# Six instead of four products of a seven-product tile with 512-column matmuls, in an attention and MoE kernel

## The chip, the cores and the metric

The kernel runs on one core of a Trainium2 chip. The metric is the device time of one execution in microseconds (us), as the median of several runs.

## The reference, cut to what is computed

```python
def _attn_ref(q, k, v, M_prev, z_prev, beta):            # q, k, v: 4 x 8 x 576 x 64
    a = softmax(causal(q @ k.T / sqrt(D)))
    local = a @ v
    q_p = elu(q) + 1
    mem_out = (q_p @ M_prev) / (q_p @ z_prev + 1e-6)
    g = sigmoid(beta)
    return g * mem_out + (1 - g) * local

def _moe_ref(x, w_in, w_out, s, b):                      # x: 2304 x 512, w_in: 512 x 2048, w_out: 2048 x 512
    r = np.maximum(x @ w_in, 0.0)
    return (s * (r * r) + b) @ w_out
```

The result of the attention, with its heads side by side, is the x of the second part. The "second product" below is the last one, with w_out; its left operand g = s r² + b is called G here.

## The kernel before

**Stages.** The attention and most of x @ w_in run first, interleaved by a planner. Then the rest of x @ w_in runs while w_out is read and split. The relu'd result r goes to DRAM (r_d) and comes back tile by tile. The last stage, 178 of 551 us, is the second product; the change is in it alone.

**Number format.** Every float32 operand X is split into H, its rounding to the matmul format (fp32r), and L = X - H. A product of A and B is the sum of three terms, H·BH + H·BL + L·BH, all added up in PSUM.

**Tiles and products.** The second product has nine tiles of 256 tokens. Each is cut 2 x 2 (tokens in halves of 128, the 2048 inner rows in halves of 1024, the 512 outputs in halves of 256) and done by a Strassen-Winograd scheme: seven products of 128 x 1024 x 256 instead of eight, with sums of blocks before (VectorE and GpSimd) and behind (VectorE). They go in the order `SEQ = [1, 7, 5, 6, 3, 2, 4]`. A product has eight steps f of 128 inner rows. Each product has one PSUM tile `yps` of two halves of 256 columns.

**Narrow and wide.** A product outside the tuple `WIDE` (narrow) takes three matmuls of 256 columns a step, H·BH (line 810), H·BL (L811) and L·BH (L812), all into the first half of its PSUM tile. A product in `WIDE` takes two: H times BH and BL side by side, 512 columns (L808), into both halves, and L·BH (L812) into the first half. The two halves are added afterwards: `onto` in `combine` runs one VectorE add from PSUM (L819) for a narrow product and two for a wide one. Product 1 has its own two instructions (L822 on ScalarE, L823 on VectorE) whichever it is.

**Left operands.** `operand(t, m, c)` makes the left operand of product m, once for each half c of the inner rows, two products ahead of its use in program order: a block sum in place (L790 for product 5 and L792 for product 6 on VectorE; L788 for product 7 and L794 for product 3 on GpSimd, into the buffer `sum`), the cast H (L795, ScalarE), and L (L796; on GpSimd for products 1, 2 and 4, on VectorE for 7, 5, 6 and 3). The tiles `op` have eight buffers, two to a product, so the operands of four products are there at most. The block sums work in place on the tile that was loaded (`src` for even tiles, `w1H` for odd ones), so L792 of the next tile's product 6 must come behind the GpSimd L796 of its product 1, which reads the block that L792 writes over. L794 needs L792's result, and L788 must come behind the VectorE L796 of product 3, which reads `sum`.

**What sets the order.** Each engine runs its instructions in the order of its own queue. In this stage the framework's scheduler, which works from a model of the times, arranges the queues; the code's order is what it starts from. TensorE's queue follows `SEQ`.

**The sums behind.** `combine` adds products 6, 7 and 5 into the running sums when product 6 is done, then 3, 2 and 4 when each is done. The sums behind product 4 of the last tile, and the DMA of the output after them, are the last work of the kernel.

Of the kernel before, what the change touches and what calls it, by code (L numbers as in the profile page):

```python
# [171 lines left out]
def attention_moe_kernel(  # L172
# [572 lines left out]
    def b_op(m, f):  # L745
        if m in LATE:
            return late[f // 4][:, f % 4, LATE.index(m)]
        return RB[f][:, PL[m]]
# [46 lines left out]
        nc.scalar.copy(H, x)  # L795
        (nc.gpsimd if m in ONPOOL else nc.vector).tensor_sub(L, x, H.bitcast(F32))  # L796

    WIDE = (1, 6, 3, 2)

    def product(t, m):  # L800
        OPS["ps", m] = tile = ps_y.tile([128, 2, NE], F32, tag="y", name="yps")
        ps = tile[:, 0]
        for f in range(KF):
            o = OPS[t, m, f // 4]
            H, L = o[:, 0, f % 4], o[:, 1, f % 4]
            B = b_op(m, f)
            if m in WIDE:
                nc.tensor.matmul(tile, lhsT=H, rhs=B, start=f == 0, stop=False)  # L808
# [5 lines left out]
    def combine(t, m):  # L814
        Y, U = YU[t % 2]

        def onto(y, x, n):
            for h in range(2 if n in WIDE else 1):
                nc.vector.tensor_add(y, y if h else x, OPS["ps", n][:, h])  # L819
# [133 lines left out]
```

## Time and profile before

| | |
|---|---|
| median of 3 runs | 554.07 us (554.06 to 554.45) |
| the profiled execution's own time | 552.9 us |
| its span, first to last instruction | 551.1 us |
| TensorE busy | 538.8 us, 98% of the span |
| VectorE, ScalarE, GpSimd busy | 395.4, 398.7, 274.1 us |
| mean granted TensorE clock | 0.994 of full speed |
| second product on TensorE | from 369.19 to 547.4 us |

In the profile PE is TensorE's matmuls, PEld its weight loads, DVE VectorE, ACT ScalarE, POOL GpSimd, and SP the engine that issues most DMAs. L with a number is a line of the kernel. A row of the timeline has its start, its duration, the engine, line and operation, what is written and read, and in brackets how long the engine had been idle before it and which instruction ended that. A VectorE instruction may start a little before the record of the one in front ends; the time from start to start is what a queue pays.

### The profile page before, as it was taken

What the parts mean: (1) busy time and instruction counts of PE and PEld (TensorE: products, weight loads), DVE (VectorE), ACT (ScalarE), POOL (GpSimd) and SP (SyncE); (2) the same over time, 40 slices, a digit from 0 to 9 for tenths busy, and PEclk for the clock granted to TensorE, in tenths of its full rate; (3) what the DMA queues carried; (4) which work ended last, traced back from release to release, by engine and by line L of the source; (5) the groups of instructions that cost most, each with busy time, mean ns of one, the idle gap of its engine ahead of it and who ended that gap; (6) DMA issues with size and microseconds to landing.
All of it is one profiled execution on the core that took longest, in us unless ns stands there. A gap on an engine that the chain in (4) does not pass through costs nothing.

```text
span 551.1 us, 11425 instructions
## 1 busy us (share of the span) xinstructions
PE 538.8 (98%) x4070; PEld 443.4 (80%) x4070; DVE 395.4 (72%) x971; ACT 398.7 (72%) x877; POOL 274.1 (50%) x279
## 2 busy tenths in 40 slices
PE   9898899999999999999999999999999999999997
PEld 6666577777777777776788888889999999999996
DVE  5999999999765445234009979353988898898893
ACT  5998799974788747647425658968988877977940
POOL 3773344556746663454000000326597678668781
PEclk9999799999999999999999999999999999999999
DMA  5645575745454342311149474648424435344011
GB/s 183 197 142 161 196 256 162 247 154 175 118 173 124 102 133 100 122 76 46 57 132 364 159 264 130 219 164 255 150 87 145 151 104 164 116 123 156 30 39 39
DMA packets 56665, 81.50 MB, mean 148 GB/s; under 512 B 7584, under 2 KB 39072, under 8 KB 56608
## 3 DMA queue, kind: packets, MB, share of 16 engines
q1 hardware_dynamic: 54064, 78.63, 44.0%
q10 hardware_dynamic: 2544, 2.14, 1.2%
q8 instruction: 32, 0.52, 0.4%
q14 instruction: 25, 0.20, 0.1%
HBM read 57.15 MB, written 23.59 MB: 147 GB/s over the span
## 4 chain that ended last, share of the span: by engine, by line
PE 90%; DVE 6%; ACT 1%; issue 1%; POOL 1%; DVEq 0%; POOLq 0%
PE yps L808 12%; PE yps L812 11%; PE sb L383 8%; PE sb L514 7%; PE tb L580 6%; PE hps L581 5%; PE hps L580 5%; PE hps L582 5%; PE tb L463 5%; PE tb L581 5%; PE tb L582 5%; PE yps L811 5%; PE yps L810 5%; PE sb L580 2%; DVE P L390 2%; PE sb L581 1%
## 5 line engine op out<-in xcount | busy, mean ns | idle before, releaser
L402 POOL TENSOR_SCALAR P<-P,sr,omg 128x576 f32<-128x576 f32 (+4 forms) x130 | 90.0, 707 | 57.1 <-DVE sr L436 31.1
L396 ACT ACTIVATE P<-P,mn 128x64 f32<-128x64 f32 (+4 forms) x160 | 89.1, 564 | 17.7 <-DVE mn L390 17.1
L812 PE MATMUL yps<-rb,op 128*128 128x256 f32 x360 | 101.1, 281 | 0.0
L390 DVE CUSTOM_DVE_ANT_0 P<-sb,mask 128x64 f32<-128x64 f32 (+4 forms) x160 | 71.6, 485 | 22.0 <-PE sb L383 21.9
L808 PE MATMUL yps<-rb,op 128*128 128x512 f32 x216 | 76.9, 396 | 0.0
L812 PEld LDWEIGHTS yps<-rb,op 128*128 128x128 f32 x360 | 67.9, 189 | 0.0
L788 POOL TENSOR_TENSOR sum<-src 128x512 f32<-128x512 f32 x10 | 13.0, 1296 | 103.5 <-ACT src L772 88.9
L383 PE MATMUL sb<-qk 64*128 64x288 f32 (+4 forms) x384 | 60.0, 419 | 0.4 <-DVE mn L390 0.4
L796 POOL TENSOR_TENSOR op<-src,op 128x512 fp32r<-128x512 f32 x30 | 44.5, 1505 | 16.8 <-ACT op L795 16.8
L463 PEld LDWEIGHTS tb<-ident,P 64*128 64x128 f32 x928 | 38.0, 141 | 17.0 <-issue 5.3
L463 PE MATMUL tb<-ident,P 64*128 64x64 f32 x928 | 44.4, 230 | 5.2 <-DVE xs L536 1.4
L383 PEld LDWEIGHTS sb<-qk 64*128 64x128 f32 x384 | 37.6, 193 | 13.4 <-issue 6.4
L808 PEld LDWEIGHTS yps<-rb,op 128*128 128x128 f32 x216 | 40.6, 188 | 9.0
L819 DVE TENSOR_TENSOR yu<-yu,yps 128x256 f32<-128x256 f32 x90 | 36.5, 414 | 14.6 <-PE yps L812 13.6
L795 ACT CAST op<-src 128x512 fp32r<-128x512 f32 x50 | 30.1, 617 | 16.2 <-DVE src L792 8.6
L810 PE MATMUL yps<-rb,op 128*128 128x256 f32 x144 | 40.5, 281 | 0.0
L811 PE MATMUL yps<-rb,op 128*128 128x256 f32 x144 | 40.5, 281 | 0.0
L796 DVE TENSOR_TENSOR op<-sum,op 128x512 fp32r<-128x512 f32 x36 | 38.3, 1065 | 0.9 <-ACT op L795 0.8
L472 ACT COPY pt<-tb 128x512 f32<-128x512 f32 x58 | 31.3, 591 | 7.6 <-PE tb L463 7.4
L796 POOL TENSOR_TENSOR op<-w1H,op 128x512 fp32r<-128x512 f32 x24 | 35.4, 1504 | 0.0
L587 ACT ACTIVATE r<-hps 128x256 f32<-128x256 f32 x62 | 21.6, 388 | 14.7 <-DMA r_d<-r 12.3
L396 ACT ACTIVATION_READ_ACCUMULATOR P<-P,mn 128x1 f32 x160 | 31.8, 199 | 0.0
(170 smaller groups left out, 1543.9 us busy)
## 6 DMA issues: line engine op xcount, KB each, us to landing
r_d<-r SPq DMA_DIRECT2D x41, 256.0 KB, 2.6
src<-r_d SPq DMA_DIRECT2D x20, 512.0 KB, 4.7
qk<-in_qk_t_dram SPq DMA_DIRECT2D x15, 576.0 KB, 4.0
raw<-in_moe_w_out_dram SPq DMA_DIRECT2D x16, 512.0 KB, 6.8
w1H<-r_d SPq DMA_DIRECT2D x16, 512.0 KB, 4.7
xa<-in_moe_w_in_dram SPq DMA_DIRECT2D x12, 512.0 KB, 4.7
r_d<-r SPq DMA_DIRECT2D x48, 128.0 KB, 2.2
qs<-in_q_rows_dram SPq DMA_DIRECT2D x16, 320.0 KB, 3.7
```

The lines of the kernel that those rows point to most:

```text
L383: nc.tensor.matmul(at(ps, j, o, n), lhsT=qk[rs, 128 * i:128 * i + 128], rhs=qk[rs, S + 64 + c0:S + 64 + c0 + n], start=True, stop=True, ti ...
L390: nc.vector.tensor_tensor_reduce(P[:, j, PB[i] + 64:PB[i] + 64 + n], at(ps, j, o, n), m, -SCALE, 3.0e38, ALU.add, ALU.min, mn[:, j, i:i + 1])
L396: nc.scalar.activation(pt, pt, AF.Exp, scale=-1.0, bias=mn[:, j, i:i + 1], accum_out=sm[:, j, i, 0:1])
L402: e.tensor_scalar(pt, pt, sr[:, j, i:i + 1], omg[:, h:h + 1], ALU.mult, ALU.mult)
L463: nc.tensor.transpose(TB[ps[h]][:, o[h]:o[h] + 64], P[rs, j, c:c + 128], ident[rs, rs], tile_position=(64 * h, 0))
L580: nc.tensor.matmul(ps, lhsT=wH[:, p, fs], rhs=xs[:, 0], start=p == 0, stop=False)
L581: nc.tensor.matmul(ps, lhsT=wH[:, p, fs], rhs=xs[:, 1], start=False, stop=False)
L796: (nc.gpsimd if m in ONPOOL else nc.vector).tensor_sub(L, x, H.bitcast(F32))
L808: nc.tensor.matmul(tile, lhsT=H, rhs=B, start=f == 0, stop=False)
L810: nc.tensor.matmul(ps, lhsT=H, rhs=B[:, 0], start=f == 0, stop=False)
L811: nc.tensor.matmul(ps, lhsT=H, rhs=B[:, 1], start=False, stop=False)
L812: nc.tensor.matmul(ps, lhsT=L, rhs=B[:, 0], start=False, stop=f == KF - 1)
```

## The change

The tuple `WIDE` gets two more products, 7 and 4. Four products of a tile were wide before (1, 6, 3 and 2), six are wide after; product 5 stays narrow. `SEQ`, the loads and the operands are the same.

```diff
-    WIDE = (1, 6, 3, 2)
+    WIDE = (1, 7, 6, 3, 2, 4)
 
     def product(t, m):
         ...
             if m in WIDE:
                 nc.tensor.matmul(tile, lhsT=H, rhs=B, start=f == 0, stop=False)
             else:
                 nc.tensor.matmul(ps, lhsT=H, rhs=B[:, 0], start=f == 0, stop=False)
                 nc.tensor.matmul(ps, lhsT=H, rhs=B[:, 1], start=False, stop=False)
             nc.tensor.matmul(ps, lhsT=L, rhs=B[:, 0], start=False, stop=f == KF - 1)
 ...
         def onto(y, x, n):
             for h in range(2 if n in WIDE else 1):
                 nc.vector.tensor_add(y, y if h else x, OPS["ps", n][:, h])
```

TensorE has 144 matmuls and as many weight loads fewer (two products, eight steps, nine tiles); VectorE has 18 adds L819 more. GpSimd's queue is the same, and ScalarE's differs in the place of one cast.

**First place: TensorE, from product 1 to product 7 of the first tile.** Before, the last step of product 1 and the first steps of product 7:

```order
L808 MATMUL yps<-rb,op 128x512
L812 MATMUL yps<-rb,op 128x256
L810 MATMUL yps<-rb,op 128x256
L811 MATMUL yps<-rb,op 128x256
L812 MATMUL yps<-rb,op 128x256
L810 MATMUL yps<-rb,op 128x256
```

After:

```order
L808 MATMUL yps<-rb,op 128x512
L812 MATMUL yps<-rb,op 128x256
L808 MATMUL yps<-rb,op 128x512
L812 MATMUL yps<-rb,op 128x256
L808 MATMUL yps<-rb,op 128x512
L812 MATMUL yps<-rb,op 128x256
```

Two matmuls of 256 columns have become one of 512.

**Second place: VectorE's queue from the sums behind product 6 of an even tile to the block sums of the next, odd one.** The adds L819 belong to the even tile; the L796 that read `sum` make product 7's L of the odd tile (first half c, then second), the two L792 its block sums for product 6. Before:

```order
L819 TENSOR_TENSOR yu_4247<-yu_4247,yps 128x256 x5
L796 TENSOR_TENSOR op<-sum,op 128x512
L819 TENSOR_TENSOR yu_4247<-yu_4247,yps 128x256
L792 TENSOR_TENSOR w1H<-w1H 128x4x128
L796 TENSOR_TENSOR op<-sum,op 128x512
L819 TENSOR_TENSOR yu_4247<-yu_4247,yps 128x256
L792 TENSOR_TENSOR w1H<-w1H 128x4x128
L796 TENSOR_TENSOR op<-w1H,op 128x512
```

After:

```order
L819 TENSOR_TENSOR yu_4247<-yu_4247,yps 128x256 x3
L796 TENSOR_TENSOR op<-sum,op 128x512
L819 TENSOR_TENSOR yu_4247<-yu_4247,yps 128x256 x2
L792 TENSOR_TENSOR w1H<-w1H 128x4x128
L819 TENSOR_TENSOR yu_4247<-yu_4247,yps 128x256
L796 TENSOR_TENSOR op<-sum,op 128x512
L819 TENSOR_TENSOR yu_4247<-yu_4247,yps 128x256
L792 TENSOR_TENSOR w1H<-w1H 128x4x128
L796 TENSOR_TENSOR op<-w1H,op 128x512
```

Of the seven adds of this stretch six stood ahead of the first L792; five do now, and there is now an add between the first L792 and product 7's second L796 where there was none. This order stands in every even and odd tile from the third on; the first two tiles have other ones.

**Third place: VectorE's queue right behind the second.** These L796 make products 5, 6 (reading `w1H`) and 3 (reading `sum`) of the odd tile; the adds are those of products 3, 2 and 4 of the even tile. Before:

```order
L796 TENSOR_TENSOR op<-w1H,op 128x512
L819 TENSOR_TENSOR yu_4247<-yu_4247,yps 128x256
L796 TENSOR_TENSOR op<-w1H,op 128x512
L819 TENSOR_TENSOR yu_4247<-yu_4247,yps 128x256
L796 TENSOR_TENSOR op<-w1H,op 128x512
L819 TENSOR_TENSOR yu_4247<-yu_4247,yps 128x256
L796 TENSOR_TENSOR op<-w1H,op 128x512
L796 TENSOR_TENSOR op<-sum,op 128x512
```

After:

```order
L796 TENSOR_TENSOR op<-w1H,op 128x512
L819 TENSOR_TENSOR yu_4247<-yu_4247,yps 128x256 x2
L796 TENSOR_TENSOR op<-w1H,op 128x512
L819 TENSOR_TENSOR yu_4247<-yu_4247,yps 128x256
L796 TENSOR_TENSOR op<-w1H,op 128x512
L819 TENSOR_TENSOR yu_4247<-yu_4247,yps 128x256
L796 TENSOR_TENSOR op<-w1H,op 128x512
L819 TENSOR_TENSOR yu_4247<-yu_4247,yps 128x256
L796 TENSOR_TENSOR op<-sum,op 128x512
```

There are two more adds here: one behind the first L796 and one ahead of product 3's first L796.

## Rows read from the trace of the kernel before

**Rows 1.** The page, busy us of each engine, share of the span, instructions.
```profile
PE 538.8 (98%) x4070; PEld 443.4 (80%) x4070; DVE 395.4 (72%) x971; ACT 398.7 (72%) x877; POOL 274.1 (50%) x279
```

**Rows 2.** Windows, the nine tiles summed: us, then each engine's busy us.
```profile
sum 178.19, PE 178.19 PEld 165.26 DVE 144.32 ACT 136.34 POOL 122.96; mean PE 19.80 PEld 18.36 DVE 16.04 ACT 15.15 POOL 13.66
```

**Rows 3.** Windows from product to product: 1 of the first tile; 1, 7, 2, 4 of the sixth.
```profile
369.19:371.96 2.77, 2.77 (x17) 2.43 (x16) 2.41 (x5) 2.04 (x5) 0.00 (x0) 1.00 0.63 176
...
468.13:470.95 2.82, 2.82 (x18) 2.46 (x17) 2.82 (x5) 2.24 (x3) 2.04 (x2) 1.00 0.25 86
470.95:473.80 2.85, 2.85 (x26) 2.85 (x25) 2.85 (x6) 2.85 (x5) 1.20 (x1) 1.00 0.00 0
...
482.29:485.08 2.79, 2.79 (x19) 2.45 (x18) 2.69 (x7) 1.28 (x3) 2.79 (x3) 1.00 0.25 57
485.08:487.94 2.86, 2.86 (x26) 2.86 (x25) 2.01 (x3) 1.59 (x2) 2.26 (x2) 1.00 0.82 250
...
sum 19.81, PE 19.81 PEld 18.37 DVE 17.18 ACT 16.45 POOL 14.70; mean PE 2.83 PEld 2.62 DVE 2.45 ACT 2.35 POOL 2.10
```

**Rows 4.** The page, groups by line: count, busy us, mean ns, then idle before.
```profile
L808 PE MATMUL yps<-rb,op 128*128 128x512 f32 x216 | 76.9, 396 | 0.0
...
L810 PE MATMUL yps<-rb,op 128*128 128x256 f32 x144 | 40.5, 281 | 0.0
```

**Rows 5.** Timeline of VectorE, end of the sixth tile and most of the seventh.
```profile
486.13 1.76 DVE L792 TENSOR_TENSOR src<-src 128x512 f32<-128x512 f32 x1 [0.85 <-POOL op L796]
487.82 0.68 DVE L796 TENSOR_TENSOR op<-sum,op 128x512 fp32r<-128x512 f32 x1
488.42 0.41 DVE L819 TENSOR_TENSOR yu<-yu,yps 128x256 f32<-128x256 f32 x1
488.75 1.45 DVE L792 TENSOR_TENSOR src<-src 128x512 f32<-128x512 f32 x1
...
491.06 1.45 DVE L796 TENSOR_TENSOR op<-src,op 128x512 fp32r<-128x512 f32 x1
...
494.30 0.68 DVE L796 TENSOR_TENSOR op<-sum,op 128x512 fp32r<-128x512 f32 x1
...
495.23 1.67 DVE L796 TENSOR_TENSOR op<-sum,op 128x512 fp32r<-128x512 f32 x1
...
505.92 1.77 DVE L792 TENSOR_TENSOR w1H<-w1H 128x512 f32<-128x512 f32 x1 [0.86 <-POOL op L796]
```

**Rows 6.** Timeline of GpSimd, the same stretch.
```profile
484.36 1.74 POOL L796 TENSOR_TENSOR op<-src,op 128x512 fp32r<-128x512 f32 x1
...
488.04 1.62 POOL L794 TENSOR_TENSOR sum<-src,src 128x512 f32<-128x512 f32 x1 [0.69 <-DVE src L792]
490.35 1.61 POOL L794 TENSOR_TENSOR sum<-src,src 128x512 f32<-128x512 f32 x1 [0.69 <-DVE src L792]
495.06 1.29 POOL L788 TENSOR_TENSOR sum<-w1H 128x512 f32<-128x512 f32 x1 [3.10 <-DVE op L796]
496.98 1.30 POOL L788 TENSOR_TENSOR sum<-w1H 128x512 f32<-128x512 f32 x1 [0.63 <-DVE op L796]
```

**Rows 7.** Timeline of VectorE, from the first tile to the second.
```profile
389.13 0.41 DVE L819 TENSOR_TENSOR yu<-yu,yps 128x256 f32<-128x256 f32 x1
389.46 1.45 DVE L796 TENSOR_TENSOR op<-sum,op 128x512 fp32r<-128x512 f32 x1
390.83 0.68 DVE L792 TENSOR_TENSOR w1H<-w1H 128x512 f32<-128x512 f32 x1
```

**Rows 8.** Timeline of GpSimd, from the first tile to the second.
```profile
388.75 1.61 POOL L794 TENSOR_TENSOR sum<-w1H 128x512 f32<-128x512 f32 x1 [1.90 <-DVE w1H L792]
391.65 1.62 POOL L794 TENSOR_TENSOR sum<-w1H 128x512 f32<-128x512 f32 x1 [1.29 <-DVE w1H L792]
```

**Rows 9.** Timeline of VectorE, the kernel's end.
```profile
544.72 0.88 DVE L819 TENSOR_TENSOR yu<-yu,yps 128x256 f32<-128x256 f32 x2 [1.92 <-PE yps L812]
547.58 0.42 DVE L819 TENSOR_TENSOR yu<-yu,yps 128x256 f32<-128x256 f32 x1 [1.99 <-PE yps L812]
```

## The prediction

> **What bounds the kernel now.** I read the page's engine totals first: TensorE is busy for 98% of the span [rows 1], so the question is what can shorten or interrupt it. Then the windows, tile by tile and product by product. In the nine tiles of the second product TensorE's busy time equals the length of the stage, 178.19 us, and the matmul groups have no idle time ahead of them [rows 2, 4]; a steady tile takes 19.81 us at the full granted clock [rows 3]. So today the stage is as long as its matmuls. VectorE is second, with 17.18 of 19.81 us in a steady tile, GpSimd has 14.70 [rows 3]. The timelines of these two show what an average does not: they work hand in hand in a ring that is as long as a tile (below).
>
> **What TensorE saves.** A step has 768 columns either way; only the cut differs. Product 7 takes 2.85 us narrow, product 4 2.86; a wide one takes 2.82 (product 1) or 2.79 (product 2, whose right operand lies in the same tiles as product 4's), and 2.77 at the best, in the first tile [rows 3]. I take 2.82 for product 7 and 2.79 for product 4, by the nearest rows: 0.03 + 0.07 = 0.10 us a tile, 0.9 us for nine. The bounds are 0.07 a tile (both at 2.82, 0.6 in all) and 0.17 (both at 2.77, 1.5 in all).
>
> The Trainium skill (TensorE: Matmul & The Clock Gate, Back-to-back issue gap) gives N/2.4 + 2.5 ns from start to start for an isolated stream of warm matmuls, so the joining would save one 2.5 ns a step: as an estimate from that page 144 x 2.5 ns = 0.36 us in place of 0.9. The trace's own difference is larger, 0.03 to 0.07 us in eight steps, and it is what I go by.
>
> **What VectorE pays.** Two adds more a tile. One is 0.41 us long, and the next instruction starts 0.33 us later (488.42 to 488.75) [rows 5]. At the kernel's very end the cost is plain: behind the last product there is one add of 0.42 us now, there will be two in a row, and such a pair takes 0.88 [rows 9], so +0.46 us ahead of the last output DMA; nothing hides that.
>
> Elsewhere 18 x 0.33 us would fit into VectorE's idle time of 2.6 us a tile, if it were free to shift. It isn't. Follow the ring in [rows 5, 6]. GpSimd's L796 of product 1's first half ends at 486.10; the first L792 waits for it and starts at 486.13. It ends at 487.89, L794 follows at 488.04; the second L792 ends at 490.20, the second L794 follows at 490.35 and ends at 491.96. VectorE then goes through its L796 without a gap, product 3's first one starts at 494.30, its second ends at 496.90, and GpSimd's second L788 follows at 496.98. From there GpSimd works through its six L796, and the next first L792 is back at 505.92. The ring takes 505.92 - 486.13 = 19.79 us, with no wait for TensorE on it, against 19.81 for TensorE's tile. It has no slack worth the name; it merely keeps pace. What stands between is a reserve: product 1's first L is done at 486.10 and its matmul starts at 487.94 [rows 3, 6], 1.84 us, the shortest such lead that I find. A ring that is longer than the tile uses that up and then stops TensorE once a tile.
>
> **What the new order does to the ring.** One thing is needed for this: a VectorE instruction with both inputs in SBUF (L790, L792, L796) takes 0.68 us, but one that starts beside a GpSimd instruction ends 0.55 us after it. L796 at 491.06 ends at 492.51, L794 at 491.96; L796 at 389.46 ends at 390.91, L794 at 390.36 [rows 5 to 8]. An add from PSUM doesn't: 0.41 us at 488.42, in the middle of an L794 [rows 5, 6].
>
> Second place of the order: behind the first L792 there is now an add ahead of product 7's second L796. That L796 started at 487.82, ahead of L794 (488.04), and went through in 0.68 us. It will be ready at 487.82 + 0.33 = 488.15, after L794 has begun. L794 ends at about 489.34 (1.30 us, as L788 alone), the L796 at 489.89, an add follows, and the second L792 runs from 490.14 to 490.82: 0.62 us later than 490.20. The trace has this very sequence once, from the first tile to the second: add, L796 of 1.45 us beside L794, L792 of 0.68 [rows 7, 8]. The second L794 starts 0.62 us later. The two adds behind it stand ahead of an L796 that waits for L794 in any case, so they are hidden. The new add ahead of product 3's L796 isn't: VectorE has no gap there, +0.33. The ring's way through GpSimd is unchanged. Sum: **0.95 us more a round**, 20.74 against a tile of 19.71.
>
> If the L796 still got in first at 488.15 (the margin is 0.11 us), this part would cost 0.33 instead of 0.62, and the round 0.66. That is the lower price of this mechanism; nothing is the lowest, if something gives way that the rows don't show.
>
> The Trainium skill (SBUF — State Buffer, Who interferes with whom) says that VectorE with two SBUF inputs shares a port with GpSimd, and that whichever issues first keeps the other out. That is the case with the 0.62; the 0.55 us in the rows agree with it, and the 0.41 us of the adds agree with its clause that one SBUF input does not contend.
>
> **The sum.** The first round (first to second tile) keeps the old places, with one add more: 0.33. Six rounds follow until product 1 of the ninth tile: 0.33 + 6 x 0.95 = 6.03 us late. TensorE, if it never waited, would be there 8 x 0.10 = 0.8 us earlier. The reserve is 1.84. TensorE waits 6.03 + 0.8 - 1.84 = 5.0 us, ahead of product 1 of the fifth to the ninth tile. In all -0.9 + 0.46 + 5.0 = **+4.6 us**. The profiled execution (552.9 us, span 551.1) would become about 557.5; the median of the runs is 1.2 us above it, so 554.07 + 4.6 = 558.7 us, and I say 558.6. The second tile's order differs from the later ones; if its round costs only 0.33, it is 558.0. With 0.66 a round: 0.33 + 6 x 0.66 + 0.8 - 1.84 = 3.25, +2.8, 556.9.
>
> **Rivals.**
> 1. *The adds find room* (other side: not slower). If the ring has a give that these rows don't show, for instance another order of turns between VectorE and GpSimd, TensorE never waits: -0.9 + 0.46 = -0.4, 553.6 us; with the bounds of the saving, 553.0 to 553.9. For it: VectorE's 2.6 us and GpSimd's 5 us idle in a tile, and that a ring exactly as long as the tile would be a coincidence unless something ties it to TensorE; I find no such tie. It decides as long as the ring grows by less than about 0.15 us a round, since the reserve then lasts to the end (7 x 0.15 + 0.8 = 1.85).
> 2. *Only the add ahead of product 3 counts*, 0.33 a round, the place beside L792 being made up for: 7 x 0.33 + 0.8 - 1.84 = 1.3, so +0.8, 554.9 us.
> 3. *Something else becomes late*: PSUM tiles, which are freed by adds that come later, or the output DMAs. Against it: there are eight PSUM tiles for seven products, and no row of before has TensorE waiting for one [rows 4]; I give it little.
>
> **How the numbers follow.** A difference of 0.2%, 1.1 us, is about what a measurement of this kernel can tell from none: the line lies at 552.96 and 555.18 us. The ring grown by 0.95: 0.46 (557.6 to 559.4). Grown by 0.66: 0.15 (556 to 557.6). Rival 2: 0.12, nearly half of it above 555.18 by its own spread. Rival 1: 0.20, a little of it below 552.96. The rest, rival 3 among it: 0.07, mostly slower. That makes slower 0.46 + 0.15 + 0.04 + 0.02 = 0.67, faster 0.05, and 0.28 between. The range must reach rival 1's value to leave out no more than 0.2: 553.4 to 559.4; the likeliest case alone has 556.9 to 559.4.
>
> **What would show it.** Right: the stage's matmuls fall from 1,224 to 1,080; product 7 at 2.82 and product 4 at 2.79; L819 at 108 instead of 90; idle time on TensorE ahead of L808 of product 1, released by GpSimd's L796, about 1 us in each of the last five tiles and none in the first three; product 7's second L796 at some 1.7 us in place of 0.68; first L792 to first L792 20.7 us. Wrong: no idle time in the matmul groups, with first L792s still 19.7 to 19.8 us apart (then the ring was tied to TensorE after all); or a wait ahead of another product.

## The result, and the profile after

| | before | after |
|---|---|---|
| median | 554.5 us (6 runs, 554.06 to 555.92) | 558.56 us (6 runs, 557.73 to 562.06) |
| profiled execution, span | 552.9, 551.1 us | 558.38, 556.6 us |
| second product on TensorE | 178.19 us | 182.17 us |

The kernel is slower: 1.0069 times the time of before, 95% interval 1.0041 to 1.0097. Of the 5.5 us between the two spans 4.0 lie in the second product and 0.5 behind it. The last 1.0 lies ahead of it, where the program is the same. The stage starts at 369.19 us in the execution of before and between 369.7 and 372.8 in those of all other kernels below, two without the change among them (second buffer in the kernel before 370.4, shorter tile 372.8). So that part is no effect of the change, and the experiments are compared by the length of the stage.

The page after, engine totals and three of the groups:

```profile
PE 541.9 (97%) x3926; PEld 435.7 (78%) x3926; DVE 397.5 (71%) x989; ACT 396.8 (71%) x877; POOL 269.9 (48%) x279
...
L808 PE MATMUL yps<-rb,op 128*128 128x512 f32 x288 | 102.2, 396 | 0.0
...
L819 DVE TENSOR_TENSOR yu<-yu,yps 128x256 f32<-128x256 f32 x108 | 42.9, 411 | 11.1 <-PE yps L812 10.3
...
L796 DVE TENSOR_TENSOR op<-sum,op 128x512 fp32r<-128x512 f32 x36 | 47.3, 1318 | 1.0 <-ACT op L795 0.8
```

There are 144 matmuls fewer than in [rows 1] and 18 adds more. The L796 that read `sum` now take 1,318 ns on average, against 1,065 in the page before, for the same work:

```profile
L796 DVE TENSOR_TENSOR op<-sum,op 128x512 fp32r<-128x512 f32 x36 | 38.3, 1065 | 0.9 <-ACT op L795 0.8
```

The windows of five tiles and the sum over all nine (us, then the engines' busy us, as in [rows 2, 3]):

```profile
409.49:429.17 19.68, 19.68 (x123) 17.54 (x122) 17.44 (x23) 16.22 (x23) 13.64 (x11) 1.00 0.38 120
429.17:449.66 20.49, 20.41 (x122) 17.51 (x121) 16.43 (x26) 16.21 (x23) 14.12 (x11) 1.00 0.39 127
...
470.14:490.90 20.76, 20.41 (x123) 17.52 (x121) 16.67 (x26) 16.21 (x23) 14.38 (x11) 1.00 0.40 127
490.90:511.64 20.74, 20.39 (x123) 17.51 (x121) 16.64 (x26) 16.21 (x23) 14.36 (x11) 1.00 0.41 126
...
532.42:552.37 19.95, 19.95 (x122) 17.46 (x120) 16.82 (x27) 4.84 (x9) 10.54 (x7) 1.00 0.13 40
sum 182.17, PE 180.96 PEld 157.62 DVE 145.05 ACT 134.66 POOL 121.02; mean PE 20.11 PEld 17.51 DVE 16.12 ACT 14.96 POOL 13.45
```

The third tile shows what the matmuls alone need, 19.68 us against 19.81 [rows 3]. From the fourth to the eighth a tile takes 20.5 to 20.8. TensorE's busy time hides most of it (20.39 of 20.74), because the profile's ends of matmuls are modelled; the length of the window is what counts. VectorE is less busy in these tiles than before (16.6 of 20.7 us against 17.18 of 19.81): it isn't short of time.

What the weight loads (PEld) and the matmuls of the second product waited for in all (us, times, longest):

```profile
PEld yps L812 <- POOL op L796: 5.4, 15, 0.6
PEld yps L812 <- DVE op L796: 0.2, 1, 0.2
```

```profile
PE yps L812 <- POOL op L796: 0.9, 3, 0.3
```

So it is GpSimd's L that is late, for L·BH; H is there in time. One such place, TensorE in the seventh tile, where product 2 begins:

```profile
505.02 0.39 PE L808 MATMUL yps<-w0H,op 128*128 128x512 f32 x1
505.71 0.39 PE L812 MATMUL yps<-w0H,op 128*128 128x256 f32 x1 [0.31 <-POOL op L796]
```

H·(BH, BL) of the first step runs at 505.02, and L·BH starts at 505.71, 0.69 us later, where 0.23 is usual. The L that it needs is the first that GpSimd makes behind its second L788; it is done at 505.66:

```profile
503.89 1.77 POOL L796 TENSOR_TENSOR op<-src,op 128x512 fp32r<-128x512 f32 x1
```

The ring after the change, VectorE and then GpSimd, to be laid beside [rows 5, 6]:

```profile
490.85 1.76 DVE L792 TENSOR_TENSOR src<-src 128x512 f32<-128x512 f32 x1 [1.78 <-POOL op L796]
492.53 0.41 DVE L819 TENSOR_TENSOR yu<-yu,yps 128x256 f32<-128x256 f32 x1
492.86 1.73 DVE L796 TENSOR_TENSOR op<-sum,op 128x512 fp32r<-128x512 f32 x1
494.52 0.41 DVE L819 TENSOR_TENSOR yu<-yu,yps 128x256 f32<-128x256 f32 x1
494.85 0.68 DVE L792 TENSOR_TENSOR src<-src 128x512 f32<-128x512 f32 x1
...
496.72 1.12 DVE L796 TENSOR_TENSOR op<-src,op 128x512 fp32r<-128x512 f32 x1
...
499.62 0.41 DVE L819 TENSOR_TENSOR yu<-yu,yps 128x256 f32<-128x256 f32 x1
499.96 0.68 DVE L796 TENSOR_TENSOR op<-sum,op 128x512 fp32r<-128x512 f32 x1
...
511.60 1.76 DVE L792 TENSOR_TENSOR w1H<-w1H 128x512 f32<-128x512 f32 x1 [1.78 <-POOL op L796]
```

```profile
492.75 1.29 POOL L794 TENSOR_TENSOR sum<-src,src 128x512 f32<-128x512 f32 x1 [0.69 <-DVE src L792]
495.67 1.61 POOL L794 TENSOR_TENSOR sum<-src,src 128x512 f32<-128x512 f32 x1 [1.63 <-DVE src L792]
500.71 1.29 POOL L788 TENSOR_TENSOR sum<-w1H 128x512 f32<-128x512 f32 x1 [3.43 <-DVE op L796]
502.63 1.30 POOL L788 TENSOR_TENSOR sum<-w1H 128x512 f32<-128x512 f32 x1 [0.63 <-DVE op L796]
```

From the start of the first L792 to the second L794 it is 4.82 us (4.22 before), to product 3's first L796 9.11 (8.17), to the second L788 11.78 (10.85), and to the next first L792 20.75 (19.79). Of the growth of 0.96 us, 0.94 is there by the time of product 3's first L796; the rest of the round only passes it on. The L796 of product 7 takes 1.73 us beside L794 where it took 0.68 ahead of it [rows 5].

One round went the other way that the prediction had left open. In the fifth tile the same L796 got in ahead of L794, and the second L792 was the one held. VectorE, then GpSimd:

```profile
449.61 1.76 DVE L792 TENSOR_TENSOR src<-src 128x512 f32<-128x512 f32 x1 [1.78 <-POOL op L796]
...
451.62 0.68 DVE L796 TENSOR_TENSOR op<-sum,op 128x512 fp32r<-128x512 f32 x1
...
452.56 1.45 DVE L792 TENSOR_TENSOR src<-src 128x512 f32<-128x512 f32 x1
```

```profile
451.80 1.66 POOL L794 TENSOR_TENSOR sum<-src,src 128x512 f32<-128x512 f32 x1 [0.98 <-DVE yu L819]
```

The next first L792 is at 470.10: this round took 20.49 us. It was not the L796 that came sooner; it starts 2.01 us behind the first L792 in both rounds. L794 came later, 2.19 us behind the first L792 and not 1.90. It does so in the fifth tile of the kernel before, too, whose first L792 starts at 446.48:

```profile
448.69 1.33 POOL L794 TENSOR_TENSOR sum<-src,src 128x512 f32<-128x512 f32 x1 [1.00 <-DVE src L792]
```

It is 2.20 or 2.21 us in the fifth tile of the second profile of the change, too, and of the first four experiments below, and 1.90 to 1.93 in the sixth to ninth tile of all of these. So this isn't chance from one execution to the next; what holds L794 there is not shown.

And the kernel's end, against [rows 9]:

```profile
552.57 0.88 DVE L819 TENSOR_TENSOR yu<-yu,yps 128x256 f32<-128x256 f32 x2 [1.94 <-PE yps L812]
```

### The profile page after: what moved, and what is told of

It is laid out like the page before. It is cut to its first block, busy times and chain, and to the rows that moved or that the text cites. A ratio compares the mean times of both kernels' runs of the same rounds, so it can differ in the third digit from the quotient of the medians.

```text
span 556.6 us, 11161 instructions
## 1 busy us (share of the span) xinstructions
PE 541.9 (97%) x3926; PEld 435.7 (78%) x3926; DVE 397.5 (71%) x989; ACT 396.8 (71%) x877; POOL 269.9 (48%) x279
## 4 chain that ended last, share of the span: by engine, by line
PE 55%; DVE 20%; POOL 11%; issue 6%; ACT 4%; DMA 2%; SPq 0%; ACTq 0%; DVEq 0%; POOLq 0%
DVE op L796 9%; POOL op L796 9%; PE sb L383 7%; PE sb L514 7%; PE tb L580 6%; PE tb L581 5%; PE tb L582 5%; PE tb L463 5%; DVE yu L819 3%; PE hps L580 3%; PE hps L581 3%; PE hps L582 3%; PE yps L808 2%; POOL sum L788 2%; DVE P L390 2%
## 5 line engine op out<-in xcount | busy, mean ns | idle before, releaser
L402 POOL TENSOR_SCALAR P<-P,sr,omg 128x576 f32<-128x576 f32 (+4 forms) x130 | 88.8, 697 | 59.8 <-DVE sr L436 18.8
L808 PE MATMUL yps<-rb,op 128*128 128x512 f32 x288 | 102.2, 396 | 0.0
L812 PE MATMUL yps<-rb,op 128*128 128x256 f32 x360 | 101.2, 281 | 0.0
L812 PEld LDWEIGHTS yps<-rb,op 128*128 128x128 f32 x360 | 67.8, 188 | 0.3 <-DVE op L796 0.2
L808 PEld LDWEIGHTS yps<-rb,op 128*128 128x128 f32 x288 | 54.1, 188 | 12.6
L788 POOL TENSOR_TENSOR sum<-src 128x512 f32<-128x512 f32 x10 | 13.0, 1297 | 102.8 <-ACT src L772 86.8
L796 POOL TENSOR_TENSOR op<-src,op 128x512 fp32r<-128x512 f32 x30 | 44.1, 1493 | 18.8 <-ACT op L795 18.8
L819 DVE TENSOR_TENSOR yu<-yu,yps 128x256 f32<-128x256 f32 x108 | 42.9, 411 | 11.1 <-PE yps L812 10.3
L796 DVE TENSOR_TENSOR op<-sum,op 128x512 fp32r<-128x512 f32 x36 | 47.3, 1318 | 1.0 <-ACT op L795 0.8
L796 POOL TENSOR_TENSOR op<-w1H,op 128x512 fp32r<-128x512 f32 x24 | 35.9, 1525 | 0.0
L795 ACT CAST op<-w1H 128x512 fp32r<-128x512 f32 x40 | 23.7, 615 | 14.4 <-DVE w1H L792 10.6
L580 PE MATMUL tb<-xs,w0H 128*128 128x512 f32 x72 | 30.2, 420 | 1.2 <-ACT pt L472 1.2
```

What stands on the lines that cost most here:

```text
L402: e.tensor_scalar(pt, pt, sr[:, j, i:i + 1], omg[:, h:h + 1], ALU.mult, ALU.mult)
L580: nc.tensor.matmul(ps, lhsT=wH[:, p, fs], rhs=xs[:, 0], start=p == 0, stop=False)
L812: nc.tensor.matmul(ps, lhsT=L, rhs=B[:, 0], start=False, stop=f == KF - 1)
```

## The experiments

Two theories stand. **The ring**: what counts is where an add stands in VectorE's queue, since the ring of VectorE and GpSimd had no slack and makes TensorE wait when it is longer than a tile. **The amount**: VectorE has too much work, and each add costs alike. The stage's length is that of the second product in the profiled execution; the ratio is to the kernel before on the same chip. Edits are shown against the kernel after the change where the text does not name the kernel before.

| run | ratio, 95% interval | stage, us (178.19 before) | first L792 to first L792, us |
|---|---|---|---|
| only product 7 | 0.9993, 0.998 to 1.0006 | 178.03 | 19.8 |
| only product 4 | 1.0025, 1.0011 to 1.004 | 179.69 | 20.3 |
| matmuls only | 1.0078, 1.0055 to 1.0101 | 180.34 | 20.7 |
| adds only | 1.0035, 1.0021 to 1.005 | 179.49 | 20.2 |
| second buffer | 0.9996, 0.9981 to 1.0011 | 177.05 | 19.7 |
| second buffer, kernel before | 1.0009, 0.9995 to 1.0023 | 178.20 | 17.6 to 20.7 |
| second buffer, last product 4 narrow | 0.9978, 0.9963 to 0.9994 | 177.14 | 19.7 |
| the change again | 1.0078, 1.0065 to 1.0091 | 182.20 | 20.7 |
| shorter tile | 0.9968, 0.9954 to 0.9982 | 176.34 | 19.8 |

**Only product 7.**

```diff
-    WIDE = (1, 7, 6, 3, 2, 4)
+    WIDE = (1, 7, 6, 3, 2)
```

> Of the two products only 7 is made wide. Theory (the ring: it matters where an add stands in VectorE's queue): the added add stands ahead of the first L792, where VectorE has 0.86 us idle in rows of before, and product 7's second L796 still comes right behind that L792. The ring stays at 19.8 us, TensorE waits nowhere or under 0.5 us in all, the time is that of before within 0.3 us or 0.2 us less. Rival (the amount of VectorE work: every add a tile costs alike): one add of the two, half of the waiting, some 2.5 us of waits on TensorE and +2 us.

```profile
507.83 1.77 DVE L792 TENSOR_TENSOR w1H<-w1H 128x512 f32<-128x512 f32 x1 [0.53 <-POOL op L796]
```

The stage is 0.16 us shorter, TensorE waits nowhere in it, and the ring stays at 19.8 us. The added add takes its 0.33 us out of VectorE's idle time ahead of the first L792, 0.53 us now and 0.86 before [rows 5]. An add that stands where VectorE idles anyway is free; the amount theory would have it cost 2 us.

**Only product 4.**

```diff
-    WIDE = (1, 7, 6, 3, 2, 4)
+    WIDE = (1, 6, 3, 2, 4)
```

> Of the two products only 4 is made wide. Theory (ring): the added add stands between the two L796 of product 6, behind the second L792, where VectorE has no gap: 0.33 us a round, the ring 20.1 us. 7 x 0.33 + 8 x 0.08 (TensorE earlier) - 1.7 of reserve = 1.2 us of waits; with 0.46 at the end and 0.7 saved, +1.0 us on before. Rival (amount): 2.5 us of waits as for e1, +2.3 us with the end.

The ring takes 20.3 us; the stage is 1.5 us longer, 2.0 with the end. That is more than the ring's 1.0 and near the rival's 2.3, so this run alone doesn't decide. The round grew by 0.45 rather than 0.33, and the timeline shows why: the added add stands right behind another one.

```profile
476.81 0.86 DVE L819 TENSOR_TENSOR yu<-yu,yps 128x256 f32<-128x256 f32 x2
477.59 0.68 DVE L796 TENSOR_TENSOR op<-w1H,op 128x512 fp32r<-128x512 f32 x1
```

The pair takes 0.78 us from start to start, where one add takes 0.33. With 0.45 in place of 0.33 the sum of the expectation gives 7 x 0.45 + 0.64 - 1.7 = 2.1 us of waits; the weight loads waited 2.3.

**Matmuls only.** The second halves of products 7 and 4 are not added, so H·BL of these two is missing from the result.

```diff
-            for h in range(2 if n in WIDE else 1):
+            for h in range(2 if n in (1, 6, 3, 2) else 1):
```

> Six products wide as in the change, but the second halves of products 7 and 4 are not added: H times BL of these two is left out of the result. VectorE has as many adds as before. Their places differ, though: one stands between the first L792 and product 7's second L796. Theory (ring): that L796 is then held beside L794, and the second L792 ends 0.3 us later, ring 20.1 us; 6 x 0.3 + 0.8 - 1.7 = 0.9 us of waits against 1.0 saved, so the time of before within 0.4 us. Rival (amount): no add more, no wait, -1.0 us.

Both expectations fail, the rival's worse: no add more than before, and yet a stage 2.2 us longer (3.3 longer than that of the second-buffer run below, whose TensorE has the same matmuls and never waits) and a median of 558.63 us (555.58 to 559.46; the profiled execution is the fastest of four). VectorE's timeline says why:

```profile
487.64 1.77 DVE L792 TENSOR_TENSOR src<-src 128x512 f32<-128x512 f32 x1 [1.79 <-POOL op L796]
489.34 0.41 DVE L819 TENSOR_TENSOR yu<-yu,yps 128x256 f32<-128x256 f32 x1
489.67 1.73 DVE L796 TENSOR_TENSOR op<-sum,op 128x512 fp32r<-128x512 f32 x1
491.32 0.68 DVE L792 TENSOR_TENSOR src<-src 128x512 f32<-128x512 f32 x1
491.93 0.41 DVE L819 TENSOR_TENSOR yu<-yu,yps 128x256 f32<-128x256 f32 x1
492.26 1.73 DVE L796 TENSOR_TENSOR op<-src,op 128x512 fp32r<-128x512 f32 x1
```

The place that I had reckoned with is there (0.41, then 1.73). There is a second one that I had overlooked in this queue: an add behind the second L792, too, so that product 5's first L796 comes after the second L794 and is held another time. The first place costs 0.29 us up to the second L794 (at 492.15), about as expected; the second costs 0.61 from there to product 3's first L796 (at 496.71). TensorE's waits are at L812 of product 5 and, in the ninth tile, of product 3 as well here: 2.1 us of its weight loads' waits are released by a VectorE L796. Only the matmuls differ from the kernel before, so it is the scheduler that moved the adds; what in its model made it do so is not shown. So the ring grows to that of the change, 20.7 us, with the adds of the kernel before.

**Adds only.** The matmuls of before; the first half of products 7 and 4 is added twice, so these count double in the result.

```diff
-            if m in WIDE:
+            if m in (1, 6, 3, 2):
 ...
-                nc.vector.tensor_add(y, y if h else x, OPS["ps", n][:, h])
+                nc.vector.tensor_add(y, y if h else x, OPS["ps", n][:, h if n in (6, 3, 2) else 0])
```

> Matmuls as before (four products wide), but products 7 and 4 are added twice: their first half counts double, so the sums are others. VectorE has the 18 adds more. One stands ahead of the first L792, one ahead of product 3's first L796; between the first L792 and product 7's second L796 there is none. Theory (ring): 0.33 us a round, ring 20.1 us, 7 x 0.33 - 1.7 = 0.6 us of waits, 0.46 at the end, +1.1 us. Rival (amount): the same 18 adds as in the change, the same waits of 4 to 5 us and the same end, +4.5 us or more, since nothing is saved on TensorE.

The same 18 adds as in the change cost 1.3 us in the stage and 0.5 behind it, not 4.5 or more. The ring is 20.2 us, 0.35 longer, with one add on it that isn't hidden. This run and the last one leave nothing of the amount theory: 18 adds in other places cost 1.8 us where the change costs 4.5, and no added add at all, in bad places, cost 3.3 us of waits.

**Second buffer.** Product 3's block sums get a buffer of their own, in room that lay idle, so that L788 need not wait for product 3's L796. The queues of VectorE and GpSimd are those of the change.

```diff
-    SUM = []
+    SUM, SUM3 = [], []
 ...
-        x = {1: a11, 7: SUM[c], 5: a21, 6: a11, 3: SUM[c], 2: a12, 4: a22}[m]
+        x = a11 if m in (1, 6) else {7: SUM, 3: SUM3}[m][c] if m in (7, 3) else {5: a21, 2: a12, 4: a22}[m]
 ...
+    w1L = wpool.tile([128, 4096], F32, tag="w1L", name="yu1")
+    SUM3.extend(w1L[:, 2048 + 512 * c:2560 + 512 * c].rearrange("p (f e) -> p f e", e=128) for c in range(2))
```

> The change with a second buffer for the block sums of product 3 (in room that lay idle), so that L788 for product 7 no longer waits for the L796 of product 3; every queue in the change's order, all 18 adds in their places. Theory (ring): L788 moves up by up to 3.4 us, the ring has slack again, it follows TensorE's tile of 19.7 us, no waits: -1.0 saved, +0.5 at the end, 0.5 us less than before and 4.5 less than the change. Rival (amount, or lock between VectorE and GpSimd in general): VectorE's and GpSimd's work is unchanged, so the waits stay, +3 to +4 us on before.

The waits on TensorE are gone, all 5 us of them: stage 177.05, every tile from the third on 19.68 us, with the same work on VectorE and GpSimd. VectorE's timeline shows the two instructions still in the unlucky turn, and GpSimd's waits that L788 no longer waits for VectorE:

```profile
487.85 0.68 DVE L792 TENSOR_TENSOR src<-src 128x512 f32<-128x512 f32 x1
488.45 0.41 DVE L819 TENSOR_TENSOR yu<-yu,yps 128x256 f32<-128x256 f32 x1
488.78 1.67 DVE L796 TENSOR_TENSOR op<-sum,op 128x512 fp32r<-128x512 f32 x1
```

```profile
POOL sum L788 <- ACT src L772: 2.5, 1, 2.5
```

The L796 is held nearly as long as in the change (1.67 us, 1.73 there), the adds stand where they stood; what was taken away is one link of the ring, and that is enough. The median is that of before: 1.1 us saved in the stage, 0.5 paid at the end. The windows of products 7 and 4 in the sixth tile, without waits:

```profile
471.72:474.55 2.83, 2.83 (x19) 2.46 (x18) 2.83 (x6) 2.77 (x4) 2.78 (x2) 1.00 0.00 0
485.82:488.59 2.77, 2.77 (x19) 2.44 (x18) 2.77 (x5) 1.58 (x2) 0.89 (x1) 1.00 0.49 166
```

**Second buffer in the kernel before**, the same edit.

> The kernel before with the same second buffer. Theory: TensorE doesn't wait there, so nothing to win: the time of before within 0.3 us, but GpSimd's wait for L796 ahead of L788 gone and the lead of product 1's first L over its matmul up from 1.84 us to 3 or more. Rival: if TensorE were held up in ways that the rows don't show, it becomes faster by over 1 us.

The stage is 178.20 us, tile for tile that of before: TensorE wasn't held up there. GpSimd waits for ScalarE's L772 ahead of L788 now and no longer for VectorE, and the two L that it makes ahead of the seventh tile are done at 484.14 us, 5.1 us ahead of the matmul at 489.20 that opens product 1.

**Second buffer, and the last product 4 narrow.** Beside the edit of the second buffer:

```diff
+    wide = lambda t, m: m in WIDE and (t, m) != (NPT - 1, 4)
 ...
-            if m in WIDE:
+            if wide(t, m):
 ...
-            for h in range(2 if n in WIDE else 1):
+            for h in range(2 if wide(t, n) else 1):
```

> The change with the second buffer, and in the last tile product 4 narrow, so that one add stands behind the last matmul as before. Theory: 1.0 us less than before by the matmuls, no waits, no cost at the end (0.2%, at the edge of what can be told). Rival (the saving of the wide matmuls is an effect of the records): the time of before.

552.96 us, 0.9978 of before: the only version with wide products 7 and 4 that is faster than before. The stage is 1.05 us shorter; the interval of the ratio allows 0.3 to 2.1 us, so the 0.9 us that the prediction had put down for TensorE is within it, and no more can be told from the times.

**The change again.**

> The change itself beside the three others, for the comparison on one chip. Theory and rival: +4 us on before, 5 us of waits on TensorE.

558.66 us; the stage within 0.03 us of the first profile, one round of 20.5 us among rounds of 20.7 included.

**Shorter tile.** The kernel before with four matmuls of a tile left out (H·BL of product 4 in four steps, missing from the result).

```diff
-                nc.tensor.matmul(ps, lhsT=H, rhs=B[:, 1], start=False, stop=False)
+                if m != 4 or f not in (4, 5, 6, 7):
+                    nc.tensor.matmul(ps, lhsT=H, rhs=B[:, 1], start=False, stop=False)
```

> The kernel before, with H times BL of product 4 left out in its last four steps (the result lacks these terms): TensorE's tile has four matmuls of 256 columns fewer, 19.81 - 0.48 = 19.33 us. VectorE's queue from the first L792 to product 3's last L796 is that of before; one add more stands between the two L790. Theory (the ring takes 19.8 us by itself, and that this equals TensorE's tile is a coincidence): first L792 to first L792 stays at 19.8 us, TensorE waits once the reserve of some 1.8 us is used up, 8 x 0.48 - 1.8 = 2.0 us of waits, so the kernel gets 4.3 - 2.0 = 2.3 us faster. Rival (the ring is tied to TensorE and follows it): first L792s 19.33 us apart, no waits, 4.3 us faster.

The windows of the third, sixth and seventh tile, and two first L792 of VectorE's timeline:

```profile
411.36:430.69 19.33, 19.33 (x134) 17.89 (x133) 15.37 (x23) 16.21 (x23) 13.02 (x10) 1.00 0.38 124
470.28:490.08 19.80, 19.80 (x135) 17.93 (x133) 16.05 (x23) 16.21 (x23) 14.69 (x11) 1.00 0.43 132
490.08:509.89 19.81, 19.80 (x134) 17.92 (x133) 16.07 (x23) 16.21 (x23) 14.69 (x11) 1.00 0.43 131
```

```profile
470.56 1.75 DVE L792 TENSOR_TENSOR w1H<-w1H 128x512 f32<-128x512 f32 x1 [2.10 <-POOL op L796]
...
490.38 1.76 DVE L792 TENSOR_TENSOR src<-src 128x512 f32<-128x512 f32 x1 [2.11 <-POOL op L796]
```

```profile
PEld yps L813 <- POOL op L796: 2.7, 11, 0.3
```

The matmuls need 19.33 us a tile, and the early tiles take that; once the reserve is gone every tile but the last takes the ring's 19.8, and the weight loads for L·BH (L813 in this kernel) wait for GpSimd. The stage is 1.85 us shorter instead of 4.3. The ring has a length of its own; that it equalled TensorE's tile before was a coincidence.

## Why the prediction was right, step by step

- **TensorE's saving**, 0.10 us a tile forecast: 0.12, as the second-buffer run shows without waits (product 7 2.85 to 2.83 us, product 4 2.87, 2.86 by the window in [rows 3], to 2.77), and 1.1 us for nine. By the isolated gap of N/2.4 + 2.5 ns in the Trainium skill (TensorE: Matmul & The Clock Gate, Back-to-back issue gap) the estimate would have been 0.36 us; the trace decides for three times that.
- **The end**, 0.46: the pair of adds takes 0.88 us in place of 0.42, and the span behind the last matmul is 0.5 longer.
- **The ring grown by 0.95 a round**: of the six rounds that this was forecast for, five grew by 0.91 to 0.96 us and one, the fifth tile's, by 0.66; the first round grew by 0.33, as forecast. In the round shown the 0.96 are made of the parts that were forecast, 0.60 at product 7's L796 and 0.34 at the add ahead of product 3. The L796 comes behind L794 by 0.11 us, the margin that was reckoned with. The Trainium skill's clause that the first to issue keeps the other out (SBUF — State Buffer, Who interferes with whom) fits both kinds of round.
- **The waits**, 5.0 us in all: 4.0 us of longer stage and 1.1 saved make 5.1. That the sum comes so close is in part luck. Up to the ninth tile's first L792 the rounds grew by 5.68 us and not 6.03, and TensorE's head start there is 1.0 us and not 0.8. The ninth tile's product 1 starts 162.22 us into the stage, against 157.37 in the second-buffer run, so TensorE has waited 4.85 us by then; 0.27 more come in the ninth tile, 0.17 of it at product 3, and the forecast had none there. The reserve of 1.84 us was read at the wrong matmul, too: L is first needed at L812, 0.23 us behind that L808.
- **The place of the waits was wrong**; it is one of the prediction's own signs of being wrong, a wait ahead of another product. I had them ahead of product 1's L808 from the fifth tile on. They are at L812 of product 2 (0.6 us in the fourth and fifth tile, 0.9 in the next three) and a little at product 4 (0.18), from the fourth tile on. I had looked for the shortest lead of before, 1.84 us at product 1, and not for which operand of the late round TensorE needs first. GpSimd makes product 2's L first in its run after L788; when TensorE has waited for it, product 1's lead is restored. And L comes late alone, so L812 waits and not L808. The sum hardly suffered.
- **Rival 1** asked for a tie between ring and TensorE. The shorter tile shows that there is none. **Rival 2**, only the add ahead of product 3, is what the adds-only run does (20.2 us a round), not the change.
- The medians are 4.06 us apart and 4.6 was forecast; the difference lies within the scatter of the runs.

## What to carry to other kernels

An engine's idle share says little about what a few more instructions cost; see on which side of a wait they will stand, and walk once round the ring of engines that wait for each other, with the new order in hand. Where a ring is as long as the bound, look for the link that is there only because a buffer is used twice: here one buffer of 4 KB a partition was worth 5 us of waits, and the matmul change paid off only with it and with one narrow product at the very end. And a scheduler that orders by a model of times moves instructions on engines that an edit doesn't touch, so two edits may not add up: alone, product 7 took 0.16 us off the stage and product 4 added 1.5, and together they added 4.0.

## What was not expected

- Matmuls alone, without one add more, lengthened the ring as much as the whole change (20.7 us), by moving adds in VectorE's queue.
- A VectorE instruction with two SBUF inputs of 128x512 that meets a GpSimd instruction takes up to 1.8 us instead of 0.68. Which of the two goes first was worth 0.3 us a round here, and both turns are in one execution, one of them only in the fifth tile.
- In the run with the matmuls only the profiled execution (555.58 us) is the fastest of four; the others take 557.95 to 559.46. The waits in its profile account for the 555.58 and not for the median of 558.63. Only one execution was profiled, so what the others spend their time on stays open. Executions of one kernel lie 2.4 to 4.3 us apart in most of the other runs, too.
